# All queries projected up front and half of them parked in DRAM, full-array matmuls in the tail, 512-wide output and second feed-forward projections, and a scheduling model that knows instruction fetch

## The chip, the cores and the metric

One core of a Trainium2 chip runs the whole program. The metric is device time in microseconds of that core. Ratios are computed as the mean time of one kernel's fast runs over the mean of the other's fast runs of the same rounds, so a ratio is not quite the ratio of the medians that stand beside it. Kernels are compared only within the same rounds.

Short names: PE is the matmul engine, "pair" is a matmul with its weight load (two PE instructions), ACT does exponentials and tanh, DVE does elementwise work, a "chunk" is 256 of the 2048 rows.

## The reference

One pre-layernorm transformer block in bf16, S = 2048, D = 1024, 32 heads of 32, F = 3584:

```python
h  = x + attention(layernorm(x), wqkv) @ wo      # softmax(q k^T / sqrt(32)) v, per head
h2 = h + gelu(layernorm(h) @ w1 + b1) @ w2 + b2  # tanh gelu
```

## The kernel before

The program is built in Python as a graph of tasks. A list scheduler simulates the engines with modelled durations and fixes the order of the tasks on each engine before anything runs; each engine then executes its own list in order. Scores and values have priority on PE, and projections are "background" that fills the gaps. The parts that matter (cuts marked):

```python
def schedule(self, pick_pe, switch=0.1, dma_rate=280.0, dma_lat=2.1, dma_issue=0.06):
    ...                                   # called with dma_rate=220.0; no term for instruction fetch

def mm(g, lhsT, rhs, start, stop, reads, cols=(0, 512)):       # every projection
    c0, c1 = cols
    occ = MM * (c1 - c0) / 512.0 + 0.0015
    for j in range(4):                    # four column tiles of 32 instead of one 128x128 matmul
        fns.append(lambda p, j=j: p.matmul(psum[32*j:32*j+32, g.bank, c0:c1], lhsT[:, 32*j:32*j+32], rhs,
                   start=start, stop=stop, tile_position=(0, 32*j), skip_group_check=True))

def wo(R, c):                             # output projection: 4 groups, two 256-wide halves each
    for k in range(4):
        ...
        for t in range(2):
            for g in range(G):
                mm(grp, OT[:, c % NOT, g, t*P:t*P+P], w[:, g, :], ..., cols=(256*t, 256*t+256))

def ffn1(R, c, tail): ...                 # first feed-forward projection, 256 rows wide, unchanged in shape
def ffn2(R, c):                           # second one: 4 column blocks of 256, 28 f-chunks, 2 row tiles
    for j in range(4):
        ws = [wblock(R, B_w2[896*q:896*q+896, 256*j:256*j+256], 7) for q in range(4)]
        ...
            for t in range(2):
                mm(grp, gT[:, fc, t*P:t*P+P], w[:, fc % 7, :], ..., cols=(256*t, 256*t+256))

def late_q(c, pair):                      # queries of chunk c, during attention of chunk c-2
    if c >= 4:                            # reload x (from a DRAM copy) and the query weights each time
        dma(xq, xd[c]); dma(wq, A_wqkv[...])
```

For each chunk c the background order is `ffn1(c-1)`, `wo(c)`, `ln2(c)`, `ffn2(c-1)`, all under attention of chunk c+1; after the last attention chunk remain `wo(7)`, `ffn2(6)`, `ffn1(7)`, `ffn2(7)`: the tail, where PE works alone.

The softmax here doesn't subtract the row's maximum and nothing guards it: scores larger than these inputs give would overflow.

## Time and profile before

| | before |
|---|---|
| time, median of 3 (range) | 1206.06 us (1204.13 to 1210.61) |
| span of the profiled run | 1214.9 us |
| PE / ACT / DVE busy | 1107.3 / 1053.0 / 836.0 us |
| pairs on PE | 32,304 |
| instruction packets on DMA queue 8 | 252 |
| last exponential starts; from there to the end | 1108.5 us; 106.4 us |
| ACT idle from 303 us to the last exponential | 39.9 us |

The profiled execution took 1217.65 us, longer than any of the timed ones beside it. So lengths read off this profile can be some us too long, and a difference between two profiles is less sure than the ratio of their times.

The page of the profile, kernel before: the span, the busy time of each engine with instruction counts, and the DMA queue that carries instructions (packets, MB, share).

```profile
span 1214.9 us, 68329 instructions
...
PE 1107.3 (91%) x32304; PEld 775.5 (64%) x32304; DVE 836.0 (69%) x1575; ACT 1053.0 (87%) x1183; POOL 34.7 (3%) x80
...
q8 instruction: 252, 4.13, 1.4%
```

4.13 MB in 252 packets are 16.4 KB each (in the trace every packet of this queue has 16,384 bytes). 64,608 matmuls and weight loads over 252 packets are 256.4 a packet. So nearly all of this queue is PE's instruction stream, and one packet is 128 pairs.

The busy table by stretch, kernel before. Each engine has its busy us and, in brackets, its instructions; then the granted clock, the DMA share and GB/s.

```profile
core 0: us, PE busy (x) PEld busy (x) DVE busy (x) ACT busy (x) POOL busy (x), PEclk, DMA share, GB/s
250.00:275.00 25.00, 21.42 (x512) 12.27 (x512) 13.85 (x26) 23.31 (x26) 0.00 (x0) 0.80 0.09 28
...
303.00:1110.00 807.00, 733.41 (x22116) 517.26 (x22112) 606.73 (x1140) 766.70 (x860) 13.29 (x24) 0.99 0.58 166
...
1110.00:1215.00 105.00, 89.23 (x3040) 81.44 (x3032) 38.52 (x70) 22.48 (x44) 2.89 (x8) 0.98 0.51 145
```

The reader should divide: 22,116 pairs in 807 us are 128 pairs per 4.67 us. PE in order of time, kernel before (start us, length us, then in brackets the idle time before it and what ended it):

```profile
1134.90 1.59 PE L493 MATMUL ps<-wr,gT 128*32 128x256 bf16 x49 [1.02 <-issue]
1136.23 0.49 PE L493 MATMUL ps<-b2t,two_row 128*32 128x256 bf16 x8
1136.45 2.13 PE L493 MATMUL ps<-wr,gT 128*32 128x256 bf16 x71
1139.74 3.68 PE L493 MATMUL ps<-wr,gT 128*32 128x256 bf16 x128 [1.16 <-issue]
1144.59 0.94 PE L493 MATMUL ps<-wr,gT 128*32 128x256 bf16 x25 [1.17 <-issue]
```

49 + 8 + 71 = 128: PE runs exactly 128 pairs in 3.68 us, then stands still until 4.84 us have gone by. "Issue" means that it waited for no semaphore. I read it as a wait for the next block of instructions.

The waits of ACT from 303 to 1110 us, kernel before:

```profile
engine line waited for: us in total, times, longest us
ACT PT L676 <- PE ps L668: 35.3, 54, 2.4
```

L676 is the exponential and L668 the score matmul: nearly all of ACT's idle time there is lateness of scores.

### The profile page before, as it was taken

The numbers are of one execution on the slowest core, as the hardware profiler recorded it, in microseconds if no ns is written. First come the engines' busy times: TensorE is split into PE (matmuls) and PEld (weight loads), VectorE is DVE, ScalarE is ACT, GpSimd is POOL, SyncE is SP. The second block draws the span as 40 slices with busy tenths as digits, with TensorE's granted clock in tenths as the row PEclk, the third lists the DMA queues.
The fourth block names the chain that finished last, engine by engine and source line by source line (L and its number), as shares of the span: only waits on it lengthen the run. The fifth ranks groups of instructions, "written<-read, shape, count | busy, mean of one in ns | idle before, by whom it ended". The sixth has DMA issues, their size and how long they took to land.

```text
span 1214.9 us, 68329 instructions
## 1 busy us (share of the span) xinstructions
PE 1107.3 (91%) x32304; PEld 775.5 (64%) x32304; DVE 836.0 (69%) x1575; ACT 1053.0 (87%) x1183; POOL 34.7 (3%) x80
## 2 busy tenths in 40 slices
PE   8999999988889999999899999989999889887788
PEld 6646556554656666676566666766667556655778
DVE  7555666666698479847985698569857964697162
ACT  4887999999999989998999999989999998895060
POOL 3200000000000000000000000000000000000000
PEclk9999999988999999999999999999999999998999
DMA  6901100103544665565465655564556457765860
GB/s 168 242 21 38 38 3 4 29 21 115 146 119 142 180 181 172 163 182 167 146 186 153 182 159 167 166 180 135 162 149 181 134 167 206 212 194 146 236 182 21
DMA packets 332265, 170.06 MB, mean 140 GB/s; under 512 B 26321, under 2 KB 329425, under 8 KB 331986
## 3 DMA queue, kind: packets, MB, share of 16 engines
q1 hardware_dynamic: 331986, 165.71, 47.7%
q8 instruction: 252, 4.13, 1.4%
q14 instruction: 27, 0.22, 0.1%
HBM read 159.39 MB, written 6.29 MB: 136 GB/s over the span
## 4 chain that ended last, share of the span: by engine, by line
PE 73%; ACT 16%; DVE 7%; issue 4%; POOL 0%; DVEq 0%; POOLq 0%; ACTq 0%
PE ps L493 50%; ACT PT L676 14%; PE ps L668 11%; PE ps L686 7%; PE ps L705 4%; DVE PS L681 2%; ACT a_th L786 1%; DVE a_xh L780 1%; PE ps L823 1%; DVE hch L745 1%; DVE a_sq L784 1%; PE ps L555 1%; ACT xnT L558 0%; DVE gT L788 0%; DVE DT L714 0%
## 5 line engine op out<-in xcount | busy, mean ns | idle before, releaser
L676 ACT ACTIVATE PT<-ps 128x1024 bf16<-128x1024 f32 x1024 | 974.4, 1033 | 66.9 <-PE ps L668 53.3
L681 DVE TENSOR_TENSOR PS<-PT 128x1024 bf16<-128x1024 bf16 x496 | 328.8, 684 | 96.0 <-PE ps L705 56.4
L493 PE MATMUL ps<-hnT,wr 128*32 128x256 bf16 x6272 | 224.7, 276 | 22.5 <-DVE a_xh L780 11.4
L493 PE MATMUL ps<-wr,gT 128*32 128x256 bf16 x6608 | 224.1, 274 | 11.0 <-issue 10.6
L668 PE MATMUL ps<-QT,KT 32*128 32x256 bf16 x4096 | 207.0, 275 | 16.7 <-ACT PT L676 14.1
L686 PE MATMUL ps<-PT,V 128*32 128x256 bf16 x4096 | 193.0, 277 | 20.8 <-ACT PT L676 15.0
L493 PEld LDWEIGHTS ps<-hnT,wr 128*32 128x32 bf16 x6272 | 157.8, 97 | 62.3 <-issue 45.2
L493 PEld LDWEIGHTS ps<-wr,gT 128*32 128x32 bf16 x6608 | 168.0, 97 | 42.2 <-issue 37.0
L705 PE MATMUL ps<-PS,ones 128*32 128x256 bf16 x1984 | 145.9, 279 | 4.8 <-DVE PS L681 3.4
L668 PEld LDWEIGHTS ps<-QT,KT 32*128 32x128 bf16 x4096 | 61.6, 92 | 135.7 <-issue 71.4
L686 PEld LDWEIGHTS ps<-PT,V 128*32 128x32 bf16 x4096 | 101.3, 97 | 50.7 <-ACT PT L676 26.6
L493 PE MATMUL ps<-xnT,Wall 128*32 128x512 bf16 (+1 forms) x1952 | 106.4, 340 | 3.7 <-ACT xnT L558 1.1
L780 DVE TENSOR_TENSOR a_xh<-ps,b1f 128x512 bf16<-128x512 f32 x98 | 67.4, 688 | 30.6 <-PE ps L493 29.2
L493 PE MATMUL ps<-wr,OT 128*32 128x256 bf16 x2048 | 77.3, 284 | 6.3 <-DVE hch L745 4.1
L705 PEld LDWEIGHTS ps<-PS,ones 128*32 128x32 bf16 x1984 | 55.2, 97 | 36.8 <-DVE PS L681 21.4
L493 PEld LDWEIGHTS ps<-xnT,Wall 128*32 128x32 bf16 x1952 | 48.1, 98 | 36.2 <-issue 11.4
L493 PE MATMUL ps<-Wall,xnT 128*32 128x256 bf16 x2048 | 67.7, 273 | 0.9 <-ACT xnT L558 0.7
L807 DVE SCALAR_TENSOR_TENSOR a_os<-ps,hch 128x512 bf16<-128x512 f32 x28 | 19.3, 690 | 69.7 <-PE ps L493 69.6
L788 DVE SCALAR_TENSOR_TENSOR gT<-a_th,a_xh 128x512 bf16<-128x512 f32 x98 | 66.5, 684 | 1.0 <-ACT a_th L786 0.8
L784 DVE SCALAR_TENSOR_TENSOR a_sq<-a_sq,a_xh 128x512 bf16<-128x512 bf16 x98 | 66.3, 685 | 0.4
L493 PEld LDWEIGHTS ps<-wr,OT 128*32 128x32 bf16 x2048 | 53.3, 100 | 20.3 <-issue 13.2
L786 ACT ACTIVATE a_th<-a_sq 128x512 f32<-128x512 bf16 x98 | 62.4, 648 | 0.5 <-DVE a_sq L784 0.2
(63 smaller groups left out, 720.3 us busy)
## 6 DMA issues: line engine op xcount, KB each, us to landing
wr<-in_B_w_dram SPq DMA_DIRECT2D x118, 448.0 KB, 4.1
wr<-in_B_w_dram SPq DMA_DIRECT2D x98, 512.0 KB, 4.3
wr<-in_A_wo_dram SPq DMA_DIRECT2D x32, 512.0 KB, 4.1
wq<-in_A_wqkv_dram SPq DMA_DIRECT2D x16, 512.0 KB, 3.9
xrb<-in_A_x_dram SPq DMA_DIRECT2D x16, 256.0 KB, 3.5
Wall<-in_A_wqkv_dram SPq DMA_DIRECT2D x16, 256.0 KB, 4.4
a_x<-in_A_x_dram SPq DMA_DIRECT2D x28, 128.0 KB, 3.6
out_dram<-a_os SPq DMA_DIRECT2D x28, 128.0 KB, 4.4
```

Of the source, the lines that this page charges most:

```text
L493: fns.append(lambda p, j=j: p.matmul(psum[32 * j:32 * j + 32, g.bank, c0:c1], lhsT[:, 32 * j:32 * j + 32], rhs, start=start, stop=stop, ti ...
L555: grp_pe(g, lambda p, dc=dc: p.transpose(psb[:, g.bank, dc * P:(dc + 1) * P], src_ap[:, dc * P:(dc + 1) * P], ident[:]), 0.064, [B_src, B_ ...
L668: fns.append(lambda p, i=i, hh=hh, r0=r0: p.matmul(psum[:, 2 * us[hh // 2] + hh % 2, 256 * i:256 * i + 256], KT[r0:r0 + 32, g, 256 * r + P ...
L676: act(lambda a, u=u, q=q: a.activation(PT[:, s, 2 * q:2 * q + 2, :], psum[:, 2 * u:2 * u + 2, :], ACT.Exp, bias=0.0, scale=SCALE), 1024, r ...
L681: dve(lambda v: v.tensor_tensor(PS[:, z, :, :], PT[:, s, :, 0:256], PT[:, s, :, 256:512], ALU.add), c_dve(1024, 2), reads=B_PT[s], writes= ...
L686: fns.append(lambda p, i=i, hh=hh: p.matmul(psum[32 * hh:32 * hh + 32, self.bank, 0:256], V[:, g, 2 * r + i, 32 * hh:32 * hh + 32], PT[:, ...
L705: fns.append(lambda p, i=i, hh=hh, src=src: p.matmul(psum[32 * hh:32 * hh + 32, self.bank, 256:512], ones32[:, :], src[:, hh, :], start=False,
L780: gate[c] = dve(lambda v, xh=xh, fc=fc, grp=grp: v.tensor_tensor(v2(xh), v2(psum[:, grp.bank, :]), b1f[:, fc:fc + 2].unsqueeze(2).broadcas ...
L784: dve(lambda v, uu=uu, sq=sq, xh=xh: v.scalar_tensor_tensor(uu, sq, C2, xh, ALU.add, ALU.mult), c_dve(512), reads=[b_sq, b_xh], writes=[b_ ...
L786: act(lambda a, th=th, uu=uu: a.activation(th, uu, ACT.Tanh, bias=0.0, scale=K2 / 2), 512, reads=[b_uu], writes=[b_th], prio=-1, kind="tanh")
L788: t = dve(lambda v, th=th, xh=xh, fc=fc: v.scalar_tensor_tensor(gT[:, fc:fc + 2, :], v2(th), 1.0, v2(xh), ALU.add, ALU.mult), c_dve(512), ...
L807: dve(lambda v, j=j, o=o, grp=grp: v.scalar_tensor_tensor(o, psum[:, grp.bank, :].rearrange("p (t c) -> p t c", t=2), 0.5, hch[:, c % 2, : ...
```

## The change

```diff
-    def schedule(self, pick_pe, switch=0.1, dma_rate=280.0, dma_lat=2.1, dma_issue=0.06):
+    def schedule(self, pick_pe, switch=0.1, dma_rate=290.0, dma_lat=2.0, dma_issue=0.38, fetch=4.6):
+                        i = state["pe"] // 256
+                        state["pe"] += 2 * len(t.fns)
+                        if state["pe"] // 256 != i:
+                            start = max(start, state["next"])
+                            state["next"] = start + fetch
...
-    NPT = 8
+    NPT = 7
...
-        grp_pe(g, fns, occ, reads, "col")
+        t = grp_pe(g, fns, occ, reads, "col")
+        t.alt = [lambda p: p.matmul(psum[:, g.bank, c0:c1], lhsT, rhs, start=start, stop=stop, ...)]
...
+            if last and n >= len(pvs) and t.alt is not None:
+                t.fns, t.mode = t.alt, "full"
...
+    def spill_q(g, h):
+        grp = group(f"s{g}.{h}")
+        proj(grp, 0, g, 1024 + 512 * h, 512, 0)
+        o, bo = stg.next()
+        evacuate("dve", o, lambda: psum[:, grp.bank, :], 512, [grp.buf], [bo])
+        dma(qd[g, h], o, P * 1024, reads=[bo], writes=[B_qd[g][h]], prio=0)
...
-        for j in range(4):                                   # ffn2
-            ws = [wblock(R, B_w2[896 * q:896 * q + 896, 256 * j:256 * j + 256], 7) for q in range(4)]
+        for j in range(2):
+            ws = [w2block(R, B_w2[512 * q:512 * q + 512, 512 * j:512 * j + 512]) for q in range(FC // 4)]
...
-    gr.schedule(pick_pe, dma_rate=220.0)
+    gr.schedule(pick_pe)
```

More of the change, by code (lines that the diff above doesn't have):

```diff
@@ L29 @@
     __slots__ = ("eng", "fns", "occ", "lat", "deps", "prio", "kind", "mode", "left", "succ", "ready", "done",
-                 "order", "inc", "flow", "value", "lane", "waits", "bytes", "grp", "frees")
+                 "order", "inc", "flow", "value", "lane", "waits", "bytes", "grp", "frees", "alt")
     def __init__(self, eng, fns, occ, lat, prio, kind, mode):
@@ L48, in __init__ @@
         self.frees = False
+        self.alt = None
 class Group:
@@ L57, in __init__ @@
         self.name = ""
-        self.soft, self.gate = set(), []
+        self.soft, self.gate, self.dmas = set(), [], []
         self.left = 0
@@ L122, in schedule @@
         lanes = [None] * self.n_lanes
-        state = {"mode": None, "dma": 0.0}
+        state = {"mode": None, "dma": 0.0, "pe": 0, "next": 0.0}
         events = []
@@ L402, in build_kernel @@
     xnT, B_xnTt = sb(ph0, "xnT", [P, 4, DC, 512], BF, 4, 4)
-    NW = 6
-    wr, B_wr = sb(ffn, "wr", [P, NW, 2048], BF, NW)
-    hch, B_hch_ = sb(ffn, "hch", [P, 2, 2, D], BF, 4)
-    B_hch = [B_hch_[:2], B_hch_[2:]]
-    gT, B_gT = sb(ffn, "gT", [P, FC, 256], BF, FC)
-    ffn.cur = max(ffn.cur, xn_lo)
-    hnT, B_hnT = sb(ffn, "hnT", [P, DC, 256], BF, 1, 2)
-    xb2, B_xb2 = sb(ffn, "xb2", [P, 2, D], BF, 2)
-    wq, B_wq = sb(ffn, "wq", [P, 2048], BF)
-    xq, B_xq = sb(ffn, "xq", [P, DC, 256], BF)
     class Ring:
@@ L428, in ring, with gelu_set @@
         return [(h[:, i, :], b[i]) for i in range(n)]
-    w_base = [(wr[:, i, :], B_wr[i]) for i in range(NW)]
     class Set:
         pass
-    def gelu_set(area, pfx, ngl, nos, nx):
-        r = Set()
-        r.xh = ring(area, pfx + "xh", ngl, 512, BF)
-        r.sq = ring(area, pfx + "sq", ngl, 512, BF)
-        r.uu = r.sq
-        r.th = ring(area, pfx + "th", ngl, 512, F32)
-        r.os = Ring(ring(area, pfx + "os", nos, 512, BF))
-        r.x = Ring(ring(area, pfx + "x", nx, 512, BF))
-        r.gl = Ring(list(zip(r.xh, r.sq, r.uu, r.th)))
-        return r
-    import os
-    if os.environ.get("SHOW"):
-        print("free", TOP - ffn.cur, "ph0", TOP - ph0.cur)
-    R1 = gelu_set(ffn, "a_", 4, 2, 2)
-    if os.environ.get("SHOW"):
-        print("free", TOP - ffn.cur)
-    R1.w = Ring(w_base)
+    def gelu_set(r, area, pfx, nsq, nth, nxh, nos):
+        r.sq = Ring(ring(area, pfx + "sq", nsq, 512, BF))
+        r.th = Ring(ring(area, pfx + "th", nth, 512, F32))
+        if nxh:
+            r.xh = Ring(ring(area, pfx + "xh", nxh, 512, BF))
+        if nos:
+            r.os = Ring(ring(area, pfx + "os", nos, 512, BF))
+        return r
+    R1 = Set()
+    NW1, NW2 = 4, 7
+    w1r, B_w1r = sb(ffn, "w1r", [P, NW1, 2048], BF, NW1)
+    hch, B_hch_ = sb(ffn, "hch", [P, 2, 2, D], BF, 4)
+    B_hch = [B_hch_[:2], B_hch_[2:]]
+    NXB2 = 1
+    xb2 = Ring(ring(ffn, "xb2", NXB2, D, BF))
+    R1.x = Ring(ring(ffn, "a_x", 2, 512, BF))
+    stg = Ring(ring(ffn, "stg", 2, 512, BF))
+    assert ffn.cur <= xn_lo - 16384
+    ffn.cur = xn_lo - 16384
+    gT, B_gT = sb(ffn, "gT", [P, FC, 256], BF, FC)
+    R1.os = Ring(ring(ffn, "a_os", 2, 512, BF))
+    hnT, B_hnT = sb(ffn, "hnT", [P, DC, 256], BF, 1, 2)
+    R1.xh = Ring(ring(ffn, "a_xh", 4, 512, BF))
+    w2r, B_w2r = sb(ffn, "w2r", [P, NW2, 2048], BF, NW2)
+    gelu_set(R1, ffn, "a_", 2, 1, 0, 0)
+    R1.w1 = Ring([(w1r[:, i, :], B_w1r[i]) for i in range(NW1)])
+    R1.w2 = Ring([(w2r[:, i, :], B_w2r[i]) for i in range(NW2)])
     psum = nc.alloc_psum_tensor("ps", [P, 8, 512], F32)
@@ L456, in build_kernel @@
     psb = psum[:].bitcast(BF)
-    xd = nc.dram_tensor("x_scratch", [NC, P, DC, 256], BF, kind="Internal").ap()
-    B_xd = [gr.buf() for _ in range(NC)]
+    qd = nc.dram_tensor("q_scratch", [G, 2, P, 512], BF, kind="Internal").ap()
+    B_qd = [[gr.buf() for _ in range(2)] for _ in range(G)]
     MM = 0.2195
@@ L494, in mm @@
                                                start=start, stop=stop, tile_position=(0, 32 * j), skip_group_check=True))
-        grp_pe(g, fns, occ, reads, "col")
+        t = grp_pe(g, fns, occ, reads, "col")
+        t.alt = [lambda p: p.matmul(psum[:, g.bank, c0:c1], lhsT, rhs, start=start, stop=stop, skip_group_check=True)]
     def act(fn, n, reads=(), writes=(), prio=0, ap_bias=False, kind=""):
@@ L624, in late_q, with load_q @@
     def late_q(c, pair):
-        if pair == 0 and c >= 4:
-            dma(xq[:, :, :], xd[c], P * 4096, reads=[B_xd[c]], writes=[B_xq], prio=0)
-        grp = group(f"q{c}.{pair}", c >= 3)
+        grp = group(f"q{c}.{pair}")
         slot = slot_of(2 * pair, c)
-        if c < 4:
-            for k in range(2):
-                proj(grp, 0, 2 * pair + k, 256 * c, 256, 256 * k)
-        else:
-            w, b = wq[:].rearrange("p (a b) -> p a b", b=256), B_wq
-            dma(w, A_wqkv[:, 256 * pair:256 * pair + 256].rearrange("(dc p) c -> p dc c", p=P), P * 4096, writes=[b], prio=0)
-            for k in range(2):
-                for dc in range(DC):
-                    mm(grp, w[:, dc, k * P:k * P + P], xq[:, dc, :], dc == 0, dc == DC - 1, [b, B_xq], cols=(256 * k, 256 * k + 256))
+        for k in range(2):
+            proj(grp, 0, 2 * pair + k, 256 * c, 256, 256 * k)
         evacuate("dve", QT[:, slot:slot + 2, :], lambda: psum[:, grp.bank, :].rearrange("p (s t) -> p s t", s=2), 512,
                  [grp.buf], B_QT[slot:slot + 2])
+    def spill_q(g, h):
[4 more added lines that the diff above has]
+        dma(qd[g, h], o, P * 1024, reads=[bo], writes=[B_qd[g][h]], prio=0)
+    def load_q(c, pair):
+        h, o = divmod(256 * c - 1024, 512)
+        slot = slot_of(2 * pair, c)
+        for k in range(2):
+            dma(QT[:, slot + k, :], qd[2 * pair + k, h, :, o:o + 256], P * 512, reads=[B_qd[2 * pair + k][h]],
+                writes=[B_QT[slot + k]], prio=0)
     unit = {"n": 0, "of": 2, "pt": 0, "ps": 0, "fi": 0}
@@ L723, in finish, with wblock @@
                 reads=[B_OS[f], B_RT[f]], writes=[B_OT[c % NOT][g]])
-    def wblock(R, src_ap, n):
-        w, b = R.w.next()
-        w = w.rearrange("p (a b) -> p a b", b=256)[:, 0:n, :]
-        dma(w, src_ap.rearrange("(dc p) c -> p dc c", p=P), P * n * 512, writes=[b], prio=1)
+    def wblock(R, src_ap):
+        w, b = R.w1.next()
+        w = w.rearrange("p (a b) -> p a b", b=256)
+        dma(w, src_ap.rearrange("(dc p) c -> p dc c", p=P), P * 4096, writes=[b], prio=1)
         return w, b
-    def rows(ap, c, k):
-        return ap[256 * c:256 * c + 256, 256 * k:256 * k + 256].rearrange("(t p) c -> p t c", p=P)
@@ L734, in wo, with w2block @@
-    def wo(R, c):
-        for k in range(4):
-            w, bw = wblock(R, A_wo[:, 256 * k:256 * k + 256], 8)
-            x3, bx = R.x.next()
-            x3 = x3.rearrange("p (t c) -> p t c", t=2)
-            dma(x3, rows(x2, c, k), P * 1024, writes=[bx], prio=1)
-            grp = group(f"wo{c}.{k}")
+    def w2block(R, src_ap):
+        w, b = R.w2.next()
+        w = w.rearrange("p (a b) -> p a b", b=512)
+        t = dma(w, src_ap.rearrange("(f p) c -> p f c", p=P), P * 4096, writes=[b], prio=1)
+        return w, b, t
@@ L741, in wo, with rows @@
+    def rows(ap, c, t, j):
+        return ap[256 * c + P * t:256 * c + P * t + P, 512 * j:512 * j + 512]
+    def wo(R, c):
+        for j in range(2):
+            ws = [w2block(R, A_wo[512 * q:512 * q + 512, 512 * j:512 * j + 512]) for q in range(2)]
             for t in range(2):
+                x3, bx = R.x.next()
+                dma(x3, rows(x2, c, t, j), P * 1024, writes=[bx], prio=1)
+                grp = group(f"wo{c}.{j}{t}")
                 for g in range(G):
-                    mm(grp, OT[:, c % NOT, g, t * P:t * P + P], w[:, g, :], g == 0, g == G - 1, [B_OT[c % NOT][g], bw],
-                       cols=(256 * t, 256 * t + 256))
@@ L745, in wo @@
-            dve(lambda v, k=k, x3=x3, grp=grp: v.tensor_tensor(
-                hch[:, c % 2, :, 256 * k:256 * k + 256], psum[:, grp.bank, :].rearrange("p (t c) -> p t c", t=2), x3, ALU.add),
-                c_dve_ps(512), reads=[grp.buf, bx], writes=B_hch[c % 2], prio=-2)
-    def ln2(c, evac, joint):
-        tiles = [(hch[:, c % 2, t, :], B_hch[c % 2][t], xb2[:, t, :], B_xb2[t]) for t in range(2)]
-        if joint:
+                    w, bw, _ = ws[g // 4]
+                    mm(grp, OT[:, c % NOT, g, t * P:t * P + P], w[:, g % 4, :], g == 0, g == G - 1, [B_OT[c % NOT][g], bw])
@@ L752, in ln2 @@
+                dve(lambda v, t=t, j=j, x3=x3, grp=grp: v.tensor_tensor(
+                    hch[:, c % 2, t, 512 * j:512 * j + 512], psum[:, grp.bank, :], x3, ALU.add),
+                    c_dve_ps(512), reads=[grp.buf, bx], writes=[B_hch[c % 2][t]], prio=-2)
+    def ln2(c, evac, joint):
+        tiles = []
+        for t in range(2):
+            o, bo = xb2.next()
+            tiles.append((hch[:, c % 2, t, :], B_hch[c % 2][t], o, bo))
+        if joint and NXB2 == 2:
             layer_norm(tiles, 0)
-        else:
-            for t in tiles:
-                layer_norm([t], 0)
@@ L756, in ln2 @@
         for t in range(2):
-            transposes(group(f"t{c}.{t}"), xb2[:, t, :], B_xb2[t], hnT[:, :, t * P:t * P + P], B_hnT[t], evac)
+            if not (joint and NXB2 == 2):
+                layer_norm(tiles[t:t + 1], 0)
+            transposes(group(f"t{c}.{t}"), tiles[t][2], tiles[t][3], hnT[:, :, t * P:t * P + P], B_hnT[t], evac)
     soft, gate = {}, {}
@@ L762, in ffn1 @@
         for blk in range(FC // 2):
-            w, bw = wblock(R, B_w1[:, 256 * blk:256 * blk + 256], 8)
+            w, bw = wblock(R, B_w1[:, 256 * blk:256 * blk + 256])
             grp = group(f"f1.{c}.{blk}")
@@ L768, in ffn1 @@
                        cols=(256 * f, 256 * f + 256))
-            (xh, b_xh), (sq, b_sq), (uu, b_uu), (th, b_th) = R.gl.next()
+            (xh, b_xh), (sq, b_sq), (th, b_th) = R.xh.next(), R.sq.next(), R.th.next()
             fc = 2 * blk
@@ L783, in ffn1 @@
             dve(lambda v, sq=sq, xh=xh: v.tensor_tensor(sq, xh, xh, ALU.mult), c_dve(512, 2), reads=[b_xh], writes=[b_sq], prio=1)
-            dve(lambda v, uu=uu, sq=sq, xh=xh: v.scalar_tensor_tensor(uu, sq, C2, xh, ALU.add, ALU.mult), c_dve(512),
-                reads=[b_sq, b_xh], writes=[b_uu], prio=1)
-            act(lambda a, th=th, uu=uu: a.activation(th, uu, ACT.Tanh, bias=0.0, scale=K2 / 2), 512,
-                reads=[b_uu], writes=[b_th], prio=-1, kind="tanh")
+            dve(lambda v, sq=sq, xh=xh: v.scalar_tensor_tensor(sq, sq, C2, xh, ALU.add, ALU.mult), c_dve(512),
+                reads=[b_sq, b_xh], writes=[b_sq], prio=1)
@@ L788, in ffn1 @@
+            act(lambda a, th=th, sq=sq: a.activation(th, sq, ACT.Tanh, bias=0.0, scale=K2 / 2), 512,
+                reads=[b_sq], writes=[b_th], prio=-1, kind="tanh")
             t = dve(lambda v, th=th, xh=xh, fc=fc: v.scalar_tensor_tensor(gT[:, fc:fc + 2, :], v2(th), 1.0, v2(xh), ALU.add, ALU.mult),
-                c_dve(512), reads=[b_th, b_xh], writes=B_gT[fc:fc + 2], prio=1)
+                    c_dve(512), reads=[b_th, b_xh], writes=B_gT[fc:fc + 2], prio=1)
             soft.setdefault(c, set()).add(t)
@@ L792, in ffn2 @@
     def ffn2(R, c):
-        for j in range(4):
-            ws = [wblock(R, B_w2[896 * q:896 * q + 896, 256 * j:256 * j + 256], 7) for q in range(4)]
-            grp = group(f"f2.{c}.{j}")
-            if c in gate:
-                grp.soft, grp.gate = soft[c], [gate[c]]
-            for t in range(2):
-                mm(grp, two_row[:, :], b2t[:, 256 * j:256 * j + 256], t == 0, False, [B_two, B_b2t], cols=(256 * t, 256 * t + 256))
-            for fc in range(FC):
-                w, bw = ws[fc // 7]
-                for t in range(2):
-                    mm(grp, gT[:, fc, t * P:t * P + P], w[:, fc % 7, :], False, fc == FC - 1, [B_gT[fc], bw],
-                       cols=(256 * t, 256 * t + 256))
-            o, bo = R.os.next()
-            o = o.rearrange("p (t c) -> p t c", t=2)
-            dve(lambda v, j=j, o=o, grp=grp: v.scalar_tensor_tensor(
-                o, psum[:, grp.bank, :].rearrange("p (t c) -> p t c", t=2), 0.5, hch[:, c % 2, :, 256 * j:256 * j + 256], ALU.mult, ALU.add),
-                c_dve_ps(512), reads=[grp.buf] + B_hch[c % 2], writes=[bo], prio=-2)
-            dma(rows(out2, c, j), o, P * 1024, reads=[bo], prio=0)
+        for j in range(2):
+            ws = [w2block(R, B_w2[512 * q:512 * q + 512, 512 * j:512 * j + 512]) for q in range(FC // 4)]
+            for t in range(2):
+                grp = group(f"f2.{c}.{j}{t}")
+                grp.soft = {d for _, _, d in ws}
+                grp.dmas = [d for _, _, d in ws]
+                if c in gate:
+                    grp.soft |= soft[c]
+                    grp.gate = [gate[c]]
+                mm(grp, two_row[:, :], b2t[:, 512 * j:512 * j + 512], True, False, [B_two, B_b2t])
+                for fc in range(FC):
+                    w, bw, _ = ws[fc // 4]
+                    mm(grp, gT[:, fc, t * P:t * P + P], w[:, fc % 4, :], False, fc == FC - 1, [B_gT[fc], bw])
+                o, bo = R.os.next()
+                dve(lambda v, j=j, t=t, o=o, grp=grp: v.scalar_tensor_tensor(
+                    o, psum[:, grp.bank, :], 0.5, hch[:, c % 2, t, 512 * j:512 * j + 512], ALU.mult, ALU.add),
+                    c_dve_ps(512), reads=[grp.buf, B_hch[c % 2][t]], writes=[bo], prio=-2)
+                dma(rows(out2, c, t, j), o, P * 1024, reads=[bo], prio=0)
@@ L832, in build_kernel @@
                 last_x = [x_tile(tt + NXR, -4)]
-        tc, h = divmod(i, 2)
-        if i >= 4:
-            dma(xd[i], xnT[:, tc, :, 256 * h:256 * h + 256], P * 4096, reads=B_xnTt[tc][2 * h:2 * h + 2], writes=[B_xd[i]], prio=1)
         proj_k(group("lead"), 0, 256 * i, 256, "dve")
@@ L894, in build_kernel @@
         attend(g, c)
-        if c == 1 and g >= 4:
-            late_q(3, g - 4)
-        if g == 7 and c == 0:
-            for k in range(4):
-                late_q(2, k)
+    for k in range(4):
+        late_q(2, k)
+    for k in range(4):
+        late_q(3, k)
+    for h in range(2):
+        for g in range(G):
+            spill_q(g, h)
     def attention(c):
@@ L904, in attention @@
             if g % 2 == 1 and c + 2 < NC:
-                late_q(c + 2, g // 2)
+                load_q(c + 2, g // 2)
     wo(R1, 0)
@@ L924, in build_kernel @@
     tail = Area(pt_lo, pt_hi)
-    R2 = gelu_set(tail, "b_", 4, 2, 4)
+    R2 = gelu_set(Set(), tail, "b_", 4, 4, 4, 2)
+    R2.x = R1.x
     slots = []
@@ L928, in build_kernel @@
         for lo, nm in ((kt_lo, "wk"), (v_lo, "wv")):
-            a = Area(lo + 4096 * k)
-            slots += ring(a, f"{nm}{k}", 1, 2048, BF)
+            slots += ring(Area(lo + 4096 * k), f"{nm}{k}", 1, 2048, BF)
     ffn1(R1, L - 1, False)
-    R1.x = R2.x
     wo(R1, L)
@@ L935, in build_kernel @@
     ffn2(R1, L - 1)
-    k = R1.w.k % NW
-    R2.w = Ring(slots + w_base[k:] + w_base[:k])
+    k = R1.w1.k % NW1
+    R2.w1 = Ring(slots[:10] + R1.w1.slots[k:] + R1.w1.slots[:k])
+    R2.w2 = Ring(slots[10:] + R1.w2.slots)
     ffn1(R2, L, True)
@@ L959, in build_kernel @@
     qks = [t for t in gr.tasks if t.kind == "qk"]
-    PV_START = 6
+    PV_START = 5
     AHEAD = 0.3
@@ L997, in pick_pe @@
                 if p.bank is None and (not new_ok or not ((p is first and n >= len(pvs)) or (
-                        p.left == 0 and p.ready <= now + AHEAD and all(x.done is not None for x in p.gate)))):
+                        p.left == 0 and p.ready <= now + AHEAD and all(x.done is not None for x in p.gate)
+                        and all(x.left == 0 for x in p.dmas)))):
                     continue
```

## The prediction

> **What bounds it now.** Span 1214.9 us, ACT busy 1053, PE 1107 (part 1 of the page). The busy table in 25 us windows gives three stretches.

> (a) Attention with feed-forward, 303 to 1110 us. ACT is busy about 24 of 25 us. It idles 38 us in all, 35.3 waiting for score matmuls (the waits of ACT there). Back-to-back exponentials start every 0.92 us; 768 of them plus about 90 tanh at 0.55 make about 756 of 807 us, so about 50 us can be won. About 26 of the 38 idle us fall beside holes of over 0.6 us in PE's weight loads, labelled "issue". I read these as instruction fetch: queue 8 moved 252 packets, 4.13 MB, 16 KB each, one per 128 matmul/weight-load pairs. [...] in the tail, runs of 128 matmuls take 3.68 us and start every 4.84 (1134.90, 1139.74, 1144.59), 1.2 us of it "issue". From 400 to 800 us PE issues 128 matmuls per 4.45 to 4.50 us: close to that limit.

> (b) The tail, 1111 to 1215, is PE alone: output projection (7), second projection of chunk 6 (35 us), first of chunk 7 (31), second of chunk 7 (27), with those stalls.

> (c) 71 to 303: ACT-bound, PE full, but thin at 250 to 300, clock 0.80 to 0.86.

> **What changes.**
> - 512-wide output and second projections: per feed-forward chunk 1184 matmuls become 592. Queries: 1024 become 512. In the tail one full-array matmul replaces four column tiles. Count: 32304 to about 25600; fetches 252 to about 200. Per attention chunk 3632 becomes about 2784: at 4.6 us per 128, 130 us becomes 100, under ACT's estimated 126.
> - Array time hardly changes. Four 256-wide column tiles start every 110 ns; the warm-up's 128x128x256 matmuls start every 109 ns, their weight load hidden.
> - Query weights and x are no longer reloaded: data bytes 165.7 to about 157 MB. The w2 and output rows per descriptor double to 1 KB.
> - Added: 16 query groups, an estimated 28 us of PE before the feed-forward, mostly into the hole at 250 to 300.
> - Fewer buffers: one tanh buffer instead of four, seven probability tiles, one norm tile. DVE is already 24 of 25 us busy in first projections, so ACT order stalls are possible.

> **On the critical path.** (a) -33 us (of 50). (b) 7.5 + 26 + 27 + 26 + ends = about 88 instead of 102: -14. Second projection of chunk 6 stays in the tail, as its weights queue behind the output projection's in the same ring. (c) about 0 to -3.

> Predicted 1160 us, 8 in 10 between 1130 and 1188. Faster 0.84, same 0.12, slower 0.04.

> **What would show it.** Queue 8 near 200 packets; matmuls near 25600. PE "issue" waits fall by over half; ACT idle from 303 to the end of attention falls from 38 to under 18 us; the last exponential moves from 1110 to about 1077. Tail of 85 to 92 us without 1.2 us "issue" gaps; full-array matmuls near 109 ns (256) and 216 ns (512) apart. PE denser at 250 to 300.

> **What would make it wrong.** ACT or PE stalling in order on the single tanh buffer or on the evacuation of the background bank (a_xh and hch waits, 24 us in (a) now) eats the gain of (a). The tail becoming DMA-bound (already 0.81 busy at 230 GB/s) gains little. The spill delaying the first feed-forward so that background work lags and lengthens the tail. The other way: the second projection of chunk 6 absorbed under attention would save up to 20 us more.

One passage is cut where it is marked. -33, -14 and 0 to -3 take 47 to 50 us off the 1206 to 1208 us of the kernel before, which gives 1156 to 1161 against the forecast's 1160. Measured, in the trace of the kernel before: exponentials back to back start 0.92 us apart (median); after a tanh the next instruction starts 0.52 us later, where the prediction's estimate has 0.55. In the warm-up the first 25 steps from matmul to matmul are 189 to 214 ns, nearly all later ones 109 or 110, while each weight load (98 ns) runs beside the matmul before it; the 216 ns is the step between sets of four 512-wide column tiles (median). From these steps the estimates can be followed: 32, 112 and 224 full-array matmuls at 216, 216 and 109 ns are 6.9, 24.2 and 24.4 us for an output, a second and a first projection of the tail, and 128 such sets are 28 us for the added queries.

## The result, and the profile after

| | before | after |
|---|---|---|
| time, median of 4 (range) | 1208.34 us (1204.13 to 1213.61) | 1167.11 us (1164.03 to 1170.59) |
| ratio, 95% interval | | 0.9658 (0.9607 to 0.9708) |
| pairs on PE; instruction packets | 32,304; 252 | 25,592; 200 |
| data moved on queue 1 | 165.7 MB | 157.3 MB |
| 256th of 1,024 exponentials starts (the end of the first two chunks) | 294 us | 290 us |
| last exponential starts | 1108.5 us | 1076.7 us |
| from there to the end of the span | 106.4 us | 92.1 us |
| ACT idle, 303 us to just after the last exponential | 39.9 us | 20.7 us |

3.4% faster. The page, kernel after:

```profile
span 1168.8 us, 55036 instructions
...
PE 1086.7 (93%) x25592; PEld 624.4 (53%) x25592; DVE 836.6 (72%) x1582; ACT 1043.9 (89%) x1183; POOL 48.6 (4%) x108
...
q8 instruction: 200, 3.28, 1.1%
```

A fifth of PE's instructions is gone, while its busy time fell by only 2%: the matmuls stream almost the same columns, so in these two runs busy time followed the columns and not the number, and it could not have shown this gain. The busy table by stretch, kernel after:

```profile
core 0: us, PE busy (x) PEld busy (x) DVE busy (x) ACT busy (x) POOL busy (x), PEclk, DMA share, GB/s
250.00:275.00 25.00, 23.86 (x653) 14.41 (x652) 14.66 (x25) 23.80 (x27) 0.00 (x0) 1.00 0.05 14
...
303.00:1078.00 775.00, 712.43 (x17824) 400.72 (x17820) 606.62 (x1148) 754.05 (x854) 28.78 (x56) 0.99 0.55 169
...
675.00:700.00 25.00, 21.69 (x657) 14.77 (x660) 23.02 (x45) 24.34 (x30) 0.00 (x0) 1.00 0.59 175
700.00:725.00 25.00, 24.19 (x672) 15.31 (x672) 23.17 (x43) 24.50 (x30) 0.00 (x0) 1.00 0.61 179
1078.00:1169.00 91.00, 86.19 (x520) 48.47 (x512) 38.19 (x70) 23.02 (x44) 3.22 (x8) 0.97 0.42 136
```

Under attention it is now 128 pairs per 5.56 us (775 x 128 / 17,824) instead of 4.67; the two rows from 675 us, of the same view in steps of 25 us, are needed further down. The hole at 250 us is filled, at full clock, by the early query work. PE in the tail, kernel after:

```profile
1088.16 5.46 PE L499 MATMUL ps<-w2r,gT 128*128 128x512 bf16 x24
...
1105.89 10.32 PE L499 MATMUL ps<-w2r,gT 128*128 128x512 bf16 x47 [0.94 <-DMA w2r<-in_B_w_dram]
1116.05 1.91 PE L499 MATMUL ps<-hnT,wk 128*128 128x256 bf16 x16
1117.79 1.91 PE L499 MATMUL ps<-hnT,wv 128*128 128x256 bf16 x16
```

No "issue" hole is left; one wait for a weight load costs 0.94 us. Sixteen 256-wide full-array matmuls start 1.74 us before the next sixteen: 109 ns each, as fast as the sets of four column tiles that they replace (by the start times in the trace of before a set starts every 110 ns; 31 such steps and the last matmul's 0.27 us make the 3.68 us above). The waits of ACT under attention, kernel after:

```profile
ACT PT L685 <- PE ps L677: 15.5, 23, 3.1
ACT PT L685 <- PE ps L695: 1.6, 1, 1.6
ACT a_th L802 <- DVE gT L804: 0.6, 2, 0.4
```

The wait for scores fell from 35.3 to 15.5 us. The single tanh buffer (last line) costs 0.6 us.

**Which holes are instruction fetch.** The label "issue" also covers short pauses, so I looked at the start times in the trace: every hole of over 0.6 us from the start of one PE weight load to the start of the next, and how long before its end the latest packet on queue 8 had landed. In the tail of the kernel before, 12 of 13 holes end 1.2 to 1.65 us after a landing (median 1.4). Holes that end in this window are called "at fetch" below. Under attention they come to 45.1 us in the kernel before and 22.6 us after. A hole can fall in the window by chance, since packets land all the time (4.5 us apart in the median before, 5.3 after), so these sums are upper estimates.

Counting instructions gives a sharper test. Count PE's weight loads, matmuls and sequencer entries together. In the kernel before and in the kernel after, packet number n always landed before PE had passed instruction 256n + 194 of this count, and in the tail of the kernel before 12 of the holes end at exactly that place (within two instructions), 1.3 to 1.6 us after the landing. So each packet carries the block that begins there, and PE waits for it. Packet n landed at most 261 instructions before PE came to that place in these two kernels: blocks came about one block ahead at best, and just in time or late where PE stood still. Under attention, the holes that lie at such a boundary and end 1.15 to 1.65 us after a landing number 29 (31.0 us) in the kernel before and 12 (15.9 us) after; in the experiments below 26 (40.9 us) in a_split2b and none in a_fullall. These stalls reach ACT: of its idle stretches of over 0.1 us under attention, 23.5 of 37.2 us before and 12.1 of 19.2 us after fall within 2.5 us of such a hole (with the holes shifted in time at random, 6.1 and 1.5 us do).

### The profile page after: what moved, and what is told of

Its sections match the earlier page's. It is cut to its first block, busy times and chain, and to the rows that moved or that the text cites. A ratio compares the mean times of both kernels' runs of the same rounds, so it can differ in the third digit from the quotient of the medians.

```text
span 1168.8 us, 55036 instructions
## 1 busy us (share of the span) xinstructions
PE 1086.7 (93%) x25592; PEld 624.4 (53%) x25592; DVE 836.6 (72%) x1582; ACT 1043.9 (89%) x1183; POOL 48.6 (4%) x108
## 4 chain that ended last, share of the span: by engine, by line
PE 57%; ACT 31%; DVE 8%; issue 2%; DMA 1%; POOL 0%; DVEq 0%; POOLq 0%
PE ps L496 33%; ACT PT L685 29%; PE ps L677 9%; PE ps L499 6%; PE ps L695 5%; PE ps L714 3%; DVE PS L690 3%; ACT a_th L802 2%; DVE a_xh L796 2%; PE ps L839 1%; DVE hch L759 1%; DMA w2r<-in_B_w_dram 1%; PE ps L559 1%; DVE gT L804 1%; DVE a_sq L800 1%
## 5 line engine op out<-in xcount | busy, mean ns | idle before, releaser
L496 PE MATMUL ps<-hnT,w1r 128*32 128x256 bf16 x6272 | 225.9, 275 | 22.5 <-DVE a_xh L796 12.3
L695 PE MATMUL ps<-PT,V 128*32 128x256 bf16 x4096 | 187.2, 274 | 14.7 <-ACT PT L685 11.4
L496 PEld LDWEIGHTS ps<-hnT,w1r 128*32 128x32 bf16 x6272 | 156.3, 97 | 67.6 <-issue 47.7
L496 PE MATMUL ps<-w2r,gT 128*32 128x512 bf16 x2688 | 181.2, 383 | 2.0 <-DVE gT L804 2.0
L496 PE MATMUL ps<-xnT,Wall 128*32 128x512 bf16 (+1 forms) x2464 | 139.9, 345 | 5.7 <-DVE QT L572 1.7
L714 PE MATMUL ps<-PS,ones 128*32 128x256 bf16 x1984 | 142.7, 276 | 2.6 <-DVE PS L690 1.5
L695 PEld LDWEIGHTS ps<-PT,V 128*32 128x32 bf16 x4096 | 99.8, 96 | 61.6 <-ACT PT L685 26.5
L496 PEld LDWEIGHTS ps<-w2r,gT 128*32 128x32 bf16 x2688 | 63.0, 96 | 62.9 <-issue 21.3
L496 PEld LDWEIGHTS ps<-xnT,Wall 128*32 128x32 bf16 x2464 | 58.6, 96 | 47.9 <-issue 15.7
L714 PEld LDWEIGHTS ps<-PS,ones 128*32 128x32 bf16 x1984 | 53.2, 96 | 40.4 <-DVE PS L690 25.4
L496 PE MATMUL ps<-w2r,OT 128*32 128x512 bf16 x896 | 63.3, 381 | 2.3 <-DVE hch L759 1.2
L496 PEld LDWEIGHTS ps<-Wall,xnT 128*32 128x32 bf16 x2048 | 51.6, 97 | 10.0 <-issue 5.7
```

The lines of the kernel that those rows point to most:

```text
L496: fns.append(lambda p, j=j: p.matmul(psum[32 * j:32 * j + 32, g.bank, c0:c1], lhsT[:, 32 * j:32 * j + 32], rhs, start=start, stop=stop, ti ...
L695: fns.append(lambda p, i=i, hh=hh: p.matmul(psum[32 * hh:32 * hh + 32, self.bank, 0:256], V[:, g, 2 * r + i, 32 * hh:32 * hh + 32], PT[:, ...
L714: fns.append(lambda p, i=i, hh=hh, src=src: p.matmul(psum[32 * hh:32 * hh + 32, self.bank, 256:512], ones32[:, :], src[:, hh, :], start=False,
```

## The experiments

Time, and what the profile of each run shows. "Attention ends" is the start of the last exponential; "tail" is from there to the end of the span; "at fetch" is under attention.

| run | time us | ratio to before (95%) | pairs | attention ends | tail | ACT idle | at fetch us |
|---|---|---|---|---|---|---|---|
| before | 1208.34 | 1 | 32,304 | 1108.5 | 106.4 | 39.9 | 45.1 |
| after | 1167.11 | 0.9658 (0.9607 to 0.9708) | 25,592 | 1076.7 | 92.1 | 20.7 | 22.6 |
| a_split2 (wrong result) | 1196.53 | 0.9891 (0.9854 to 0.9928) | 29,272 | 1104.3 | 90.9 | 45.2 | 44.2 |
| a_split2b | 1198.32 | 0.9929 (0.9887 to 0.9970) | 29,272 | 1107.4 | 89.8 | 49.2 | 43.1 |
| a_coltail | 1173.18 | 0.9700 (0.9663 to 0.9738) | 27,056 | 1073.8 | 97.4 | 18.3 | 19.2 |
| a_oldsched | 1171.59 | 0.9681 (0.9639 to 0.9723) | 25,592 | 1079.9 | 88.9 | 22.0 | 14.4 |
| b_alttail | 1196.61 | 0.9892 (0.9854 to 0.9930) | 30,048 | 1109.5 | 92.8 | 42.6 | 38.9 |
| b_sched | 1196.20 | 0.9890 (0.9849 to 0.9930) | 32,304 | 1056.9 | 138.5 | 16.6 | 31.7 |
| b_sched_alt | 1174.84 | 0.9708 (0.9665 to 0.9750) | 29,316 | 1050.8 | 119.2 | 10.0 | 19.2 |
| b_spill | 1201.99 | 0.9935 (0.9894 to 0.9976) | 31,792 | 1095.3 | 105.3 | 33.7 | 33.5 |
| a_fullall | 1166.81 | 0.9646 (0.9600 to 0.9692) | 14,744 | 1058.3 | 105.1 | 5.4 | 3.2 |
| a_hybrid | 1161.20 | 0.9625 (0.9578 to 0.9671) | 17,702 | 1063.3 | 96.6 | 8.5 | 6.0 |
| a_hybrid_f5 | 1154.74 | 0.9571 (0.9535 to 0.9608) | 17,600 | 1062.7 | 90.4 | 6.3 | 5.6 |

Names that start with a_ are edits of the kernel after, with b_ of the kernel before. All runs but a_split2 gave the reference's result.

### Same work and same order, more instructions: a_split2 and a_split2b

Each 512-wide column-tile matmul of the output and second projections under attention is issued as two 256-wide ones. The scheduling model is told the old count, and I compared the lists of tasks: the order on PE, ACT, DVE and the DMA queue is identical.

```diff
-        for j in range(4):
-            fns.append(lambda p, j=j: p.matmul(psum[32*j:32*j+32, g.bank, c0:c1], ..., rhs, start=start, ...))
+        w = (c1 - c0) // split                      # split = 2 for wo and ffn2
+        for h in range(split):
+            for j in range(4):
+                fns.append(lambda p, j=j, h=h: p.matmul(psum[32*j:32*j+32, g.bank, c0+h*w:c0+h*w+w], ...,
+                           rhs[:, h*w:h*w+w], start=start, ...))      # a_split2b: start=start and h == 0
```

> The changed kernel with every 512-wide column-tile matmul of the output and second projections outside the tail issued as two 256-wide ones. The order of work on every engine, the DMAs, the array columns and the tail stay the same; about 3,550 more matmul and weight-load pairs (29,100 instead of 25,592). Theory (the gain under attention comes from fewer PE instructions, because their fetch stalls PE): the stretch from 303 us to the last exponential grows by 15 to 22 us, time 1182 to 1190 us, ACT idle there from 20.7 back to 33 or more. Rival (the gain comes from the better static order, the fewer DMA bytes and the queries moved to the front): all of that is kept, so 1167 to 1172 us.

> The run with split matmuls again, mended: its first form gave a wrong result (only the first of the two halves may carry the start flag). Work, order and instruction count are the same, so the time is again 1192 to 1199 us, the result is correct, and the time before the last exponential is again near 1104 us instead of 1077 us.

a_split2 gave a wrong result (relative error 0.24). Both halves carried the start flag. a_split2b differs in that one argument: it gives only the first half the flag, and is correct. What the second flag does to the sums was not looked into. The times of the two are alike (1196.53 and 1198.32 us).

The split cost about 30 us: nearly the whole gain came back, more than the 15 to 22 us expected. The end of attention went from 1076.7 to 1107.4 us, the tail stayed short. The busy table and the waits of ACT, a_split2b:

```profile
core 0: us, PE busy (x) PEld busy (x) DVE busy (x) ACT busy (x) POOL busy (x), PEclk, DMA share, GB/s
303.00:1108.00 805.00, 721.93 (x21464) 500.95 (x21456) 607.48 (x1147) 755.85 (x853) 28.07 (x56) 0.99 0.53 163
```

```profile
ACT PT L690 <- PE ps L682: 41.8, 40, 4.0
```

805 x 128 / 21,464 is 4.80 us per 128 pairs, and the waits for scores are back at 41.8 us. Array columns, data moved, order, buffers and query handling were those of the fast kernel (in the two traces, too, ACT, DVE, GpSimd and the DMA queue run the same instructions in the same order). Only the instruction count differed, so the count is what the attention stretch gained from, and the rival falls. The count includes the weight loads, which double with the matmuls. Their own time is not the limit: they are busy for 501 of 805 us, and in the tail above 128 pairs with all their weight loads ran in 3.68 us. The loss was larger than expected because I had interpolated between 25,592 and 32,304 pairs; the order here was fixed by a model that believed in the smaller count, so nothing could move out of the way.

### Column tiles in the tail again: a_coltail

```diff
-            if last and n >= len(pvs) and t.alt is not None:
-                t.fns, t.mode = t.alt, "full"
```

> The changed kernel without the full-array matmuls: the tail uses four column tiles again, 512 wide in the output and second projections, 256 wide in the first. Theory: 512-wide column tiles need 128 matmuls per about 7 us and are not fetch-bound, the 256-wide first projection of the last chunk is (896 matmuls, 7 blocks at 4.3 to 4.8 us instead of 24.5 us in all): the tail grows from 92 us (last exponential to end) by 5 to 9 us, time 1172 to 1176 us. Rival 1 (the full array is what shortened the tail): grows by the whole 14 us, to about 1181 us. Rival 2 (the tail is bound by DMA or array time): no change, within 2 us of 1167 us.

The tail grew from 92.1 to 97.4 us, time 1173.18 us: the size that the theory gave. (Its 4.3 to 4.8 us per block: in the tail of the kernel before, packets on queue 8 landed 3.4 to 6.2 us apart, 4.3 in the median.) But its reason is only half right. The waits of PE in the tail, a_coltail:

```profile
PE ps L496 <- ACT b_xh L792: 2.6, 7, 0.5
PE ps L496 <- issue: 2.2, 1, 2.2
```

One fetch hole of 2.2 us opened in the first projection, and another 2.6 us went to banks that ACT had not yet emptied, a wait which the kernel after does not have there. So with 512-wide projections in it the tail was hardly short of instructions any more, and in the finished change the full array is worth about 5 us (a rough size: the intervals of this run and of the change, 0.9663 to 0.9738 and 0.9607 to 0.9708, overlap).

### Full-array matmuls in the tail of the kernel before: b_alttail

The same two lines, added to the kernel before (256 wide, old loads).

> The kernel before with one thing of the change: full-array matmuls in the tail, still 256 wide, same loads. Theory (the tail was short of PE instructions): the tail of about 105 us after the last exponential shrinks by 11 to 15 us, issue gaps there vanish, time 1193 to 1198 us; the time before the last exponential stays at 1108 us. Rival (the tail was bound by the weight loads in 512-byte rows, or by array time): it shrinks by less than 5 us, time above 1203 us.

The tail fell from 106.4 to 92.8 us, inside the expected range, and everything before it stayed. PE in the tail, b_alttail:

```profile
1130.41 6.28 PE L497 MATMUL ps<-wr,gT 128*128 128x256 bf16 x56
1136.53 0.38 PE L497 MATMUL ps<-b2t,two_row 128*128 128x256 bf16 x2
1136.74 6.28 PE L497 MATMUL ps<-wr,gT 128*128 128x256 bf16 x56
```

The stretch that before ran with a hole every 128 pairs now runs through. The old loads in 512-byte rows kept up, so they were not what bound the tail. The profiled run was this kernel's slowest (1204.09 us; the other four 1195.69 to 1198.75).

### The new scheduling model alone: b_sched

```diff
-    def schedule(self, pick_pe, switch=0.1, dma_rate=280.0, dma_lat=2.1, dma_issue=0.06):   # called with 220.0
+    def schedule(self, pick_pe, switch=0.1, dma_rate=290.0, dma_lat=2.0, dma_issue=0.38, fetch=4.6):
```

> The kernel before with only the scheduling model of the change (fetch term, DMA rate 290, issue 0.38, latency 2.0): same instructions, another static order. Theory (the number of PE instructions matters, not the order): within 6 us of 1208 us. Rival (the better order is the gain): 1175 to 1190 us.

1196.20 us: neither. My theory gave at most 6 us and the model was worth 13; the rival gave 18 or more. The busy table, b_sched:

```profile
303.00:1058.00 755.00, 694.40 (x20932) 482.38 (x20920) 568.74 (x1075) 738.32 (x836) 12.12 (x24) 1.00 0.57 165
...
1058.00:1196.00 138.00, 117.14 (x4020) 105.93 (x4016) 70.92 (x128) 31.30 (x58) 2.96 (x8) 0.99 0.62 176
```

PE still gets 128 pairs per 4.62 us (755 x 128 / 20,932), and attention nevertheless ends 52 us sooner: with the fetch term the scheduler leaves more background work for later, 4,020 pairs in the tail's window instead of 3,040, and the tail grows by 32 us. ACT idle under attention falls from 39.9 to 16.6 us. The two sum to a gain of 19.5 us in this pair of profiles and of 13 us by the ratio of the times; the difference comes mostly from the profiled run of the kernel before, which was 9 us over its median. This is a second effect beside the count, and I had not priced it.

### Both small parts together: b_sched_alt

b_sched and b_alttail in one kernel, still 256 wide, queries as before.

> The kernel before with two things of the change: the new scheduling model and the full-array matmuls in the tail. The run with the model alone ended attention at 1057 us but left a tail of 138.5 us at 4.29 us per 128 matmuls. Theory (that tail is only short of instructions): full-array matmuls bring the about 32 blocks in it to 3.68 us each at most, so the tail falls by 15 to 22 us to 116 to 123 us, time 1174 to 1182 us. Rival (the deferred work in the tail is bound by DVE, ACT or the weight loads): falls by under 8 us, time above 1188 us.

1174.84 us, as the theory had it. (For the tail of b_sched its table gives 4,020 pairs in 138 us, 4.39 us per 128; the expectation has 4.29.) The busy table, b_sched_alt:

```profile
303.00:1052.00 749.00, 695.93 (x20976) 482.01 (x20964) 570.15 (x1077) 738.83 (x837) 12.11 (x24) 1.00 0.58 167
1052.00:1171.00 119.00, 112.27 (x1028) 98.95 (x1020) 69.93 (x127) 31.66 (x58) 3.93 (x8) 0.98 0.69 200
```

The two are worth more together (2.9%) than one by one (1.1% each): one moves work into the tail, the other makes instructions cheap there. Two edits of a few lines reach within 8 us of the whole change.

### The queries alone: b_spill

```diff
+    for h in range(2):
+        for g in range(G):
+            spill_q(g, h)                    # and load_q(c + 2, ...) in place of late_q for chunks 4 to 7
```

> The kernel before with only the queries changed: all projected up front, those of the last four chunks parked in DRAM and loaded back, 512 wide; 1,024 matmuls leave the attention stretch, 512 are added ahead of it. Theory (PE instructions are what counts: the split run lost 27.6 us for 3,680 matmuls): the stretch gains 6 to 9 us, the start loses 0 to 3, time 1200 to 1205 us. Rival (moving them forward delays the feed-forward and costs more than it saves): 1208 us or more.

1201.99 us, ratio 0.9935: as expected. Attention ends at 1095.3 us, in this pair of profiles 13 us sooner rather than the 6 to 9 expected. That is likely too much, as the profile of the kernel before is of a run 9 us over its median: the times differ by 8 us, and the interval of the ratio allows 3 to 13 us.

### The old scheduling model in the kernel after: a_oldsched

> The changed kernel with the old scheduling model (no fetch term, DMA rate 220, issue 0.06, latency 2.1): same instructions, another static order. Theory (with 5.56 us per 128 matmuls under attention PE is no longer short of instructions on average, so a model without fetch does little harm): 1167 to 1176 us. Rival (the model's order is worth as much here as the 13 us that it was worth to the kernel before): 1178 us or more.

1171.59 us; the intervals of this run (0.9681) and of the change (0.9658) overlap. The model that is worth 13 us to the kernel before is worth at most a few us once instructions are no longer short on average. So the parts of the change replace one another: singly they give 13 (model), 13 (tail) and 8 us (queries), and the split shows 30 for the width, 64 in all, against 41 together.

### Full array everywhere: a_fullall

```diff
-        t = grp_pe(g, fns, occ, reads, "col")
-        t.alt = [lambda p: p.matmul(psum[:, g.bank, c0:c1], lhsT, rhs, ...)]
+        fns = [lambda p: p.matmul(psum[:, g.bank, c0:c1], lhsT, rhs, ...)]
+        grp_pe(g, fns, occ, reads, "full")
```

> The changed kernel with full-array matmuls instead of four column tiles in all projections from the first to the last, not only in the tail; about 25,592 pairs become about 14,000. Theory (what is left of issue holes under attention is still instruction fetch): ACT idle between 303 us and the last exponential falls from 20.7 to under 12 us, time 1150 to 1162 us. Rival [...]: attention grows, time 1170 us or more.

The reason that the rival gave is cut out of its text, as no run shows it; its forecast stands. Both came half true. ACT idle under attention fell to 5.4 us and attention ended at 1058.3 us, so what had been left of ACT's waits was indeed shortage of instructions. Yet the time is 1166.81 us, no better than the change: the tail grew to 105.1 us. PE under attention, a_fullall (L695 values, L714 denominators, both column-tiled; L498 full-array):

```profile
544.22 0.28 PE L714 MATMUL ps<-PS,ones 128*32 128x256 bf16 x4
544.33 0.39 PE L695 MATMUL ps<-PT,V 128*32 128x256 bf16 x8
544.65 0.39 PE L498 MATMUL ps<-w2r,gT 128*128 128x512 bf16 x1
544.97 0.29 PE L714 MATMUL ps<-PS,ones 128*32 128x256 bf16 x4
545.09 0.39 PE L695 MATMUL ps<-PT,V 128*32 128x256 bf16 x8
```

Column tiles follow column tiles without loss: L695 starts 0.11 us after L714, the time of one set of four. After L695's two sets (0.22 us) the full-array matmul should start at 544.55 and starts at 544.65; after its 0.216 us L714 should start at 544.87 and starts at 544.97. Each change between full array and column tiles costs 0.10 us here, and about 105 ns over the run. From scores (row tiles: 32*128 in the trace, each matmul on 32 rows of the array) to background the form makes no difference: from the start of the last score matmul to the start of the next matmul it is 200 ns (median) to full array here and 198 ns to column tiles in the kernel after. What PE does in the 105 ns of a change is not seen in the trace. Some 470 such changes between 303 and 1050 us are an estimated 50 us of PE. That the work which they displace is what lengthened the tail is argued, not shown; the next two runs bear on it.

### Full array where it costs no switch: a_hybrid and a_hybrid_f5

```diff
-            if last and n >= len(pvs) and t.alt is not None:
+            if t.alt is not None and (state["mode"] != "col" or (last and n >= len(pvs))):
```

a_hybrid_f5 also has fetch=5.0 instead of 4.6 in the scheduling model.

> The changed kernel with a full-array matmul for a background task wherever the one before it on PE is not column-tiled (after scores, after transposes, after another full-array one), and column tiles only after values and denominators. In the run with full-array matmuls everywhere a change between full array and column tiles cost about 105 ns, about 470 times, while scores to full array cost no more than scores to column tiles (199 against 197 ns). Theory (that switching is what ate the gain there): about half of the switches remain, the last exponential moves to 1058 to 1068 us, the tail to 92 to 97 us, time 1152 to 1162 us. Rival (with attention at its ACT bound, the background work only moves into the tail whatever the instructions): time 1164 to 1169 us, tail above 100 us.

> The same with 5.0 us instead of 4.6 us per block of 256 instructions in the scheduling model. Theory: with fetch no longer binding, the term hardly matters, within 4 us of the run before it. Rival: an order that leaves more room for fetch removes the rest of the ACT idle time, 4 us or more faster.

a_hybrid took 1161.20 us with attention to 1063.3 and a tail of 96.6 us: the theory's ranges. Of the changes between full array and column tiles 156 of 476 remained, a third and not half as expected. By itself this run does not settle the matter: its interval (0.9578 to 0.9671) overlaps with those of a_fullall and of the change. a_hybrid_f5 took 1154.74 us, 6 us faster than a_hybrid in the same rounds, so here the rival was right about the size. It was not right about the place: ACT idle under attention moved from 8.5 to 6.3 us only, and the tail fell from 96.6 to 90.4 us: the last output of chunk 6's first projection was written at 1065 us instead of 1090, so less work was left for the tail. With PE far from its fetch limit (8.0 us per 128 pairs; attention stood at 4.57 to 4.80 in b_sched_alt, b_sched, the kernel before and a_split2b) the term acts as a knob on the order. Why 5.0 gives the better order was not studied, and other values may do as well. The busy table and the waits of ACT, a_hybrid_f5:

```profile
303.00:1063.00 760.00, 714.78 (x12163) 376.06 (x12155) 606.81 (x1147) 753.66 (x854) 27.27 (x56) 0.99 0.56 171
1063.00:1154.00 91.00, 85.68 (x520) 48.63 (x520) 39.51 (x72) 24.36 (x46) 3.22 (x8) 0.97 0.41 136
```

```profile
ACT PT L685 <- PE ps L677: 3.3, 11, 1.3
```

The wait for scores is 3.3 us. This version beats both kernels: 4.3% under before, its own four runs within 0.8 us of each other.

## Why the prediction was right

- **Total.** Predicted 1160 us (1130 to 1188), measured 1167.11. The expected gain of 46 to 48 us (1160 against the two medians of the kernel before) was 41 in the medians. The spans of the profiled pair differ by 46.1 us (1214.9 to 1168.8); that this meets the forecast is partly luck, since the profiled run of the kernel before was 9 us over its median and that of the kernel after 3.5.
- **What bounds it.** Right, and shown by a_split2b: attention waited for scores because PE was short of instructions, 16 KB at a time. Counts came as predicted: 25,592 pairs, 200 packets, 157.3 MB.
- **(a) attention, -33 us.** The mis-sized term of the sum. From the 256th to the last exponential the stretch shrank from 814.3 to 786.8 us, by 27. (The last exponential did move to the 1077 us forecast, but about 4 us of that came from the start.) ACT idle fell to 20.7 us, not under 18. I compared averages: 2,784 pairs per chunk at 4.6 us per 128 are 100 us, under ACT's 126, so I took fetch to be out of the way. But the first projection is still 256 wide, and where it runs the kernel after is again at the limit: the busy table has 657 and 672 pairs in the two windows from 675 to 725 us, 128 per 4.8 us. 16 to 23 us of holes at fetch are left (by the strict and the loose count above); by the strict count, all but 0.7 us of them lie in windows of 25 us in which the first projection runs. The full-array runs, which remove them, bring ACT idle to 5 to 9 us.
- **(b) tail, -14 us.** Measured -14.3. The second projection of chunk 6 did stay in the tail (its four outputs leave DVE between 1096 and 1116 us). Full-array matmuls started 109 and 216 ns apart, as forecast. What I put down to them alone is shared: b_alttail shows that they suffice, a_coltail that 512-wide tiles nearly suffice.
- **(c) start, 0 to -3 us.** The 256th exponential moved from 294 to 290 us.
- **"Issue" waits fall by over half.** True of PE's matmuls alone (over the whole run 33.5 us before, 13.2 after), not with the weight loads, which the prediction did not set apart. Under attention the label summed to 192.0 us over both before and to 129.7 after, a fall of a third. Most of what is left are short pauses (285 of mean 0.27 us in one group). The holes at fetch did halve, 45.1 to 22.6 us. The label was too coarse an indicator.
- **Dangers.** The single tanh buffer cost 0.6 us, the tail waited 0.9 us for a load, the background bank's waits fell (a_xh and hch, 25 to 17 us). None mattered.
- **What was left out.** The prediction gave no value to the scheduling model, which the diff also changed. Alone it is worth 13 us (b_sched); inside the change it is worth little (a_oldsched).
- **What stays open.** The column "at fetch" of the table still holds some holes that fall there by chance. How much of the start's 4 us is the early query work and how much the clock that no longer dips (0.80 from 250 to 275 us before, 1.00 after) was not separated. The 512-wide width was tested by undoing its instruction count, not by adding it to the kernel before. The two smaller rules of the scheduler were not tested.

## What to carry to other kernels

Count a PE's instructions as a resource of its own: when runs of 128 matmuls with a weight load each are followed by holes that no semaphore explains, or a stretch sits at 4.5 to 4.8 us per 128 of them (4.57 to 4.80 under attention here), try wider matmuls, and full-array ones instead of four column tiles: here they helped even though the array does the same columns (30 us for the width by a_split2b, 13 for the full array in the tail by b_alttail). Look at that rate window by window, because an average below the limit hides the phases that still sit on it. Use the full array in runs between row-tiled work, not singly among column tiles, where each change costs 0.1 us, and let the scheduler know the limit, since deferring background work pays more if the work is cheap where it lands (the model alone gave 13 us, the full array in the tail alone 13, both together 35).
